# Moving a fold of the attention probabilities from VectorE to GpSimd in seven of eight batches

## The chip, the cores and the metric

The kernel runs on one core of one Trainium2 chip. The metric is the device time of one execution in microseconds (us), as the median of three runs. Engines are named as the profile names them: PE (TensorE matmul), PEld (TensorE weight load), DVE (VectorE), ACT (ScalarE), POOL (GpSimd), SP (SyncE, which here only starts DMAs).

## The reference, cut to what matters

The inputs are q, k, v (8 batches, 8 heads, 576 tokens, 64 values) and phi (32 memory slots for each token). An attention layer is followed by a Fourier mixing and a two-layer network:

```python
a = softmax(phi)                                 # over the 32 slots
k_m, v_m = a^T k, a^T v                          # 32 memory rows for each head
attn = softmax(q k_m^T / 8)                      # 576 x 32 for each head
x = (attn @ v_m) laid out as (8, 576, 512)
u = x + real(fft(fft(x, axis=1), axis=2))
un = (u - mean) / sqrt(var + 1e-6)
out = u + relu(un @ w_ch1) @ w_ch2               # 512 -> 2048 -> 512
```

The real part of the two-dimensional transform is made as matmuls with cosine and sine tables. Along the tokens it needs, of the probabilities `attn`, sums and differences of token t with token 576 - t, and again of those with their mirror at a quarter of the length. These sums and differences are the fold that the change is about.

## The kernel before, in words

**Two streams of work.** The network runs in 18 chunks of 256 tokens, each in 8 steps: `ffn1` (48 matmuls `ph`, 128x256) makes a slice of the hidden layer, ACT and DVE split it into two f16 halves (L940, L941, tile `hring`), and `ffn2` (24 matmuls `po`, 128x512) adds it into two PSUM banks. Chunk 0 is made in f32 with the raw weights while these are still being converted (`ffn1_direct`, `ffn2_direct`: `ph` at L894, ACT eviction L897, `po` at L911). The last chunks use another form of the second product. Beside that a generator, `background`, makes the attention and the mixing of the 8 batches, one step of it after each step of the network. Batch 0 stands before the network; batch 1 falls into chunks 0 and 1; batches 2 to 7 follow one by one until about 770 us.

**A batch of the background.** Heads are handled in four pairs. For b >= 2 `pooling_weights` turns phi into the tile `et` by way of `elt` and a DMA transpose (L419 on ACT, L420 on DVE, then `et<-elt`). Per pair `pair_memory` splits k and v into f16 halves and makes the memories (matmuls `pm`), and `pair_scores` makes the scores (matmuls `psc`) and their softmax in the tile `aring`. After the fourth pair come `values` (matmuls `pv`) and `spectrum` (matmuls `pa`, L741 and L749), then the mixing (`pp`, `px`).

**The end of `pair_scores`, which the change edits.** For b >= 1: POOL normalises (L635, 128x384); ACT and POOL make the two f16 halves of the first ten blocks (L647, L648); POOL makes the first level of the fold (L650, twice 128x128); DVE makes the second level in the tile `eo` (L652, L656, and L653, which has a per-partition mask in column 65 of `mk`); ACT casts `eo` to f16 (L659, tile `aeo`); POOL makes eight blocks of the low half (L660) and DVE the other four (L661, with the mask in column 64). The first matmul of `spectrum` reads those four blocks. In batch 0 DVE also does the work of L635 and L650.

**What sets the order.** The program is written for a scheduler that places each instruction on its engine's queue by a timeline of its own; engines then run their queues strictly in order. So an edit at one place can move rows of all engines at others.

Of the kernel before, what the change touches and what calls it, by code (L numbers as in the profile page):

```python
# [16 lines left out]
ALU = mybir.AluOpType  # L17
# [3 lines left out]
P = 128  # L21
B, H, S, D, M = 8, 8, 576, 64, 32
# [115 lines left out]
def kernel(  # L138
# [10 lines left out]
    nc = tc.nc  # L149
# [27 lines left out]
    mk = small[:, 0:68]  # L177
# [75 lines left out]
    def tiny(tag, n, bufs=2):  # L253
        if tag not in rings:
            rings[tag] = [taken[0], 0]
            taken[0] += n * bufs
        o, i = rings[tag]
        rings[tag][1] += 1
        o += i % bufs * n
        assert taken[0] <= 464, taken  # L260
        return scratch[:, o : o + n]
# [51 lines left out]
    def groups():  # L313

        last = [None]

        def mm(out, lhsT, rhs, start, stop):
            with tc.issue_after(last[0].ins) if start and last[0] is not None else nullcontext():
                m = nc.tensor.matmul(out, lhsT=lhsT, rhs=rhs, start=start, stop=stop)  # L319
            if stop:  # L320
                last[0] = marks["pe"] = m

        return mm
# [271 lines left out]
    def pair_scores(b, g, q, sc, km, es, aeo):  # L595

        n = f"{b}_{g}"
        psc = psg.tile([P, 512], F32, tag="g", name=f"psc_{n}")
        mm = groups()
        if b < NX:  # L600
            for t in range(6):
                mm(psc[:, t * 64 : t * 64 + 64], lhsT=q[:, t * P : (t + 1) * P], rhs=km, start=True, stop=True)
        else:
            nc.scalar.activation(qs[0], q, AF.Copy, scale=sc[:, 0:1])
            nc.vector.scalar_tensor_tensor(
                out=qs[1], in0=q, scalar=sc[:, 0:1], in1=qs[0], op0=ALU.mult, op1=ALU.subtract
            )
        for t in range(6) if b >= NX else ():
            for i, (qa, ka) in enumerate(((0, 0), (1, 0), (0, 1))):
                mm(  # L610
                    psc[:, t * 64 : t * 64 + 64],
                    lhsT=qs[qa][:, t * P : (t + 1) * P],
                    rhs=km[:, ka],
                    start=(i == 0),
                    stop=(i == 2),
                )
        pv = psc[:, 0:384].rearrange("p (c m) -> p c m", m=M)
        mx = tiny("smx", 12, 2)
        nc.vector.tensor_reduce(out=mx, in_=pv, axis=AX.X, op=ALU.max)  # L619
        a2, eo = aring[:, (b * NG + g) % NA], eot  # L620
        if b == 0 and g > 1:
            a2 = unring.rearrange("p a l t k c -> p (a l t k c)").bitcast(F32)[:, 640 * (g - 2) : 640 * (g - 1)]
            a2 = a2.rearrange("p (t m) -> p t m", m=M)
        if b == 0 and 0 < g < 3:
            eo = un.rearrange("p t c -> p (t c)")[:, 384 * (g - 1) : 384 * g]
            eo = eo.rearrange("p (t e c) -> p t e c", e=2, t=3)
        a = a2[:, :12]
        nc.vector.tensor_tensor(out=a, in0=pv, in1=mx.unsqueeze(2).to_broadcast([P, 12, M]), op=ALU.subtract)  # L628
        nc.scalar.activation(a, a, AF.Exp, scale=es)  # L629
        sm = tiny("ssm", 12, 2)  # L630
        nc.vector.tensor_reduce(out=sm, in_=a, axis=AX.X, op=ALU.add)
        nc.vector.tensor_scalar(out=sm, in0=sm, scalar1=1e-9, scalar2=2.0**-13, op0=ALU.add, op1=ALU.mult)
        nc.vector.reciprocal(out=sm, in_=sm)  # L633
        eng = nc.gpsimd if b else nc.vector
        eng.tensor_tensor(out=a, in0=a, in1=sm.unsqueeze(2).to_broadcast([P, 12, M]), op=ALU.mult)  # L635

        av = a.rearrange("p (t h) m -> p t (h m)", h=2)
        ahl = ahring[:, (b * NG + g) % NAH]
        if b == 0 and g > 0:
            ahl = ud.rearrange("p l t c -> p (l t c)")[:, (g - 1) * 5 * P : g * 5 * P]  # L640
            ahl = ahl.rearrange("p (t c) -> p t c", t=5)
        if b == 0:
            nc.scalar.copy(out=ahl[:, :, 0:64], in_=av[:, 0:5])
            nc.gpsimd.tensor_tensor(out=ahl[:, :, 64:128], in0=av[:, 0:5], in1=ahl[:, :, 0:64], op=ALU.subtract)
        else:
            ahl = ahs[:, g % 2]
            nc.scalar.copy(out=ahl[:, :, 0::2], in_=a[:, :10].unsqueeze(2).to_broadcast([P, 10, 2, M]))  # L647
            nc.gpsimd.tensor_tensor(out=ahl[:, :, 1], in0=a[:, :10], in1=ahl[:, :, 0], op=ALU.subtract)  # L648
        for i, op in ((12, ALU.add), (16, ALU.subtract)):
            eng.tensor_tensor(out=a2[:, i : i + 4], in0=a[:, 0:4], in1=a[:, 4:8], op=op)  # L650
        ap = a2[:, 8:].rearrange("p (t s h) m -> p t s (h m)", s=2, h=2)
        nc.vector.tensor_tensor(out=eo[:, 1:3, 0], in0=ap[:, 1:3, 0], in1=ap[:, 1:3, 1], op=ALU.add)  # L652
        nc.vector.scalar_tensor_tensor(  # L653
            out=eo[:, 0, 0], in0=ap[:, 0, 0], scalar=mk[:, 65:66], in1=ap[:, 0, 1], op0=ALU.mult, op1=ALU.add
        )
        nc.vector.tensor_tensor(out=eo[:, :, 1], in0=ap[:, :, 0], in1=ap[:, :, 1], op=ALU.subtract)  # L656
        hi, lo = (aeo[:, l].rearrange("p t e h c -> p (t e h) c")[:, :, g * M : g * M + M] for l in range(2))
        eov = eo.rearrange("p t e (h m) -> p (t e h) m", m=M)
        marks[f"a{b}_{g}"] = nc.scalar.copy(out=hi, in_=eov)  # L659
        nc.gpsimd.tensor_tensor(out=lo[:, 4:], in0=eov[:, 4:], in1=hi[:, 4:], op=ALU.subtract)  # L660
        marks[f"s{b}_{g}"] = nc.vector.scalar_tensor_tensor(  # L661
            out=lo[:, :4], in0=hi[:, :4], scalar=mk[:, 64:65], in1=eov[:, :4], op0=ALU.mult, op1=ALU.add
        )

        return ahl

# [502 lines left out]
    marks = {}  # L1169
# [6 lines left out]
    def background():  # L1176
# [3 lines left out]
        for b in range(B):  # L1180
# [7 lines left out]
            if b == 0:  # L1188

                for g in range(NG + 1):  # L1190
                    if g < NG:
                        km = memory_f32(b, g, first[g], vmf, [0])
                        mem[g] = first[g][:, KV:], None, km, 1.0 / 8.0
                    if g > 0:
                        ahl[g - 1] = pair_scores(b, g - 1, *mem.pop(g - 1), aeo)
                for g in range(NG):
                    memory_f32(b, g, first[g], vmf, [1])
            for step in range(NG + 2) if b > 0 else ():
                if step < NG:
                    r = load_pair(b, step)  # L1200
                if step >= 2:
                    pair_transpose(b, step - 2, ahl.pop(step - 2), attnT)
                if 0 <= step - 1 < NG:
                    ahl[step - 1] = pair_scores(b, step - 1, *mem.pop(step - 1), aeo)
                    yield (nt if half_made is None else half_made), 0
                if step < NG:
                    mem[step] = pair_memory(b, step, r, vmf, ivs)
                    yield (nt if half_made is None else half_made), 0
# [44 lines left out]
    for g in range(NG):  # L1253
        with tc.issue_after(marks["q"].ins):
            marks["q"] = nc.sync.dma_start(
                out=phi_next[:, :, g], in_=raw[1, g, :, KV:KVP].rearrange("p (t c) -> p t c", t=NST)
# [203 lines left out]
```

## Time and profile before

| | |
|---|---|
| median of 3 runs | 921.37 us (920.95 to 921.78) |
| the profiled execution | 921.82 us, of which the span from the first to the last instruction 920.0 us |
| PE busy | 908.0 us, 99% of the span |
| DVE, ACT, POOL busy | 618.9, 492.9, 268.4 us |
[...]

Read first how much of the span PE works, then where it waits and for whom, then the engines at those places. An engine that is half idle can still be the one that ends such a wait, since each runs its own queue in order.

### The profile page before, as it was taken

The page shows a single profiled execution, that of the slowest core. Times are in us where ns is not written, and L with a number is a line of the kernel's source. Part 1 is how long each engine was busy: PE and PEld are TensorE (multiplying, and loading weights), DVE is VectorE, ACT ScalarE, POOL GpSimd, SP SyncE. Part 2 cuts the span into 40 slices and gives each one's busy share as a digit, 9 for nine tenths or more (in the row PEclk, how much of TensorE's full clock was granted, in tenths as well). Part 3 has the DMA queues.
Part 4 walks back from the last instruction along what each step waited for, and adds up shares of the span by engine and source line. Part 5 has one row for each costly group of instructions (what it writes and reads, how often), then busy time and mean ns, then how long its engine had stood idle before and what let it go on. Part 6 is the DMA issues. An engine that isn't in the chain of part 4 may idle for free.

```text
span 920.0 us, 19352 instructions
## 1 busy us (share of the span) xinstructions
PE 908.0 (99%) x7796; PEld 670.4 (73%) x7796; DVE 618.9 (67%) x1471; ACT 492.9 (54%) x955; POOL 268.4 (29%) x302
## 2 busy tenths in 40 slices
PE   9999899999999999999999999999999999999998
PEld 8976567667766676666766667676676767688887
DVE  5979967686668766777634876766665866554554
ACT  5658867655455555655434464655556544533331
POOL 1304524232154413372160431162222421300000
PEclk9999999999999999999999999999999999999999
DMA  9958841454245261454124425165425443210000
GB/s 327 413 172 285 212 90 24 98 130 107 41 107 122 70 146 34 123 155 137 20 69 89 117 75 141 25 141 125 96 49 110 103 131 106 47 46 2 24 14 34
DMA packets 132761, 100.16 MB, mean 109 GB/s; under 512 B 115008, under 2 KB 115264, under 8 KB 130624
## 3 DMA queue, kind: packets, MB, share of 16 engines
q1 hardware_dynamic: 132672, 98.93, 40.4%
q8 instruction: 61, 1.00, 0.4%
q14 instruction: 28, 0.23, 0.1%
HBM read 62.35 MB, written 13.63 MB: 83 GB/s over the span
## 4 chain that ended last, share of the span: by engine, by line
PE 87%; DVE 6%; ACT 4%; issue 1%; DMA 1%; POOL 0%; ACTq 0%; SPq 0%; POOLq 0%
PE ph L319 36%; PE po L950 29%; PE po L1012 6%; PE pp_t L319 2%; PE pm L319 2%; PE psc L319 2%; PE po L911 1%; PE pa L749 1%; PE ph L894 1%; PE px_t L319 1%; PE idle L297 1%; PE pm L498 1%; DMA et<-elt 1%; PE pp_t L800 1%; DVE w2s L1101 1%
## 5 line engine op out<-in xcount | busy, mean ns | idle before, releaser
L319 PE MATMUL ph<-unring,w1t 128*128 128x256 f16 x3264 | 389.3, 273 | 0.0
L319 PEld LDWEIGHTS <-w1t 128*128 128x128 f16 x3264 | 313.8, 98 | 60.7 <-issue 2.7
L950 PE MATMUL po<-w2s,hring 128*128 128x512 f16 x1344 | 311.6, 379 | 0.0
L950 PEld LDWEIGHTS <-hring 128*128 128x128 f16 x1344 | 129.5, 98 | 130.7 <-issue 0.4
L941 DVE SCALAR_TENSOR_TENSOR hring<-ph,hring 128x512 f16<-128x512 f32 x112 | 76.2, 682 | 39.2 <-ACT hring L940 37.9
L940 ACT ACTIVATE hring<-ph 128x512 f16<-128x512 f32 x112 | 65.9, 588 | 48.8 <-PE ph L319 48.7
L635 POOL TENSOR_TENSOR aring<-aring,scratch 128x384 f32<-128x384 f32 x28 | 25.6, 916 | 181.7 <-DVE scratch L633 152.4
L860 POOL TENSOR_TENSOR scratch<-scratch,small 128x1 f32<-128x1 f32 x36 | 22.5, 627 | 180.9 <-DVE scratch L859 152.9
L881 POOL TENSOR_TENSOR ud<-un,ud 128x1024 f16<-128x1024 f32 x17 | 37.9, 2228 | 31.0 <-ACT ud L880 31.0
L629 ACT ACTIVATE aring<-aring,scratch 128x384 f32<-128x384 f32 x24 | 14.7, 611 | 55.7 <-DVE aring L628 55.7
L319 PEld LDWEIGHTS <-stg 128*128 128x128 f16 x912 | 35.5, 97 | 8.3 <-issue 4.0
L659 ACT CAST aeo<-eo 128x384 f16<-128x384 f32 x30 | 15.4, 512 | 43.4 <-DVE eo L656 43.4
L619 DVE TENSOR_REDUCE scratch<-psc 128x12 f32<-128x384 f32 x32 | 17.6, 551 | 26.0 <-PE pm L319 18.7
L836 DVE SCALAR_TENSOR_TENSOR uring<-px_t,scratch,share 128x256 f32<-128x256 f32 (+1 forms) x80 | 34.2, 477 | 0.9 <-PE px_t L319 0.8
L647 ACT CAST at<-aring 128x640 f16<-128x640 f32 x28 | 20.3, 724 | 25.1 <-POOL aring L635 25.1
L911 PE MATMUL po<-w2s,hring 128*128 128x512 f32 x64 | 31.2, 610 | 2.0 <-ACT hring L897 2.0
L1034 POOL TENSOR_TENSOR uring<-uring,share 128x256 f32<-128x256 f32 x3 | 2.2, 728 | 105.9 <-ACT share L1031 105.9
L650 POOL TENSOR_TENSOR aring<-aring 128x128 f32<-128x128 f32 x56 | 31.7, 586 | 2.0
L894 PE MATMUL ph<-unring,w1t 128*128 128x256 f32 x128 | 30.6, 383 | 0.0
L652 DVE TENSOR_TENSOR eo<-aring 128x128 f32<-128x128 f32 x29 | 26.7, 919 | 4.9 <-POOL aring L650 4.9
L894 PEld LDWEIGHTS ph<-unring,w1t 128*128 128x128 f32 x128 | 23.9, 190 | 7.7 <-issue 5.0
L854 ACT ACTIVATE un<-uring 128x512 f32<-128x512 f32 x32 | 20.0, 624 | 17.5 <-POOL ud L881 8.7
(324 smaller groups left out, 1544.3 us busy)
## 6 DMA issues: line engine op xcount, KB each, us to landing
out<-uring SPq DMA_DIRECT2D x35, 256.0 KB, 2.1
rawt<-in_raw SPq DMA_DIRECT2D x13, 640.0 KB, 4.5
stg<-in_raw SPq DMA_DIRECT2D x13, 640.0 KB, 5.1
stg<-in_w SPq DMA_DIRECT2D x7, 1024.0 KB, 6.4
rawt<-in_raw SPq DMA_DIRECT2D x15, 384.0 KB, 3.2
stg<-in_raw SPq DMA_DIRECT2D x15, 384.0 KB, 3.1
w2s<-in_w SPq DMA_DIRECT2D x4, 1024.0 KB, 10.5
kept_t<-ud SPq DMA_DIRECT2D x8, 512.0 KB, 2.6
```

The lines of the kernel that those rows point to most:

```text
L319: m = nc.tensor.matmul(out, lhsT=lhsT, rhs=rhs, start=start, stop=stop)
L635: eng.tensor_tensor(out=a, in0=a, in1=sm.unsqueeze(2).to_broadcast([P, 12, M]), op=ALU.mult)
L650: eng.tensor_tensor(out=a2[:, i : i + 4], in0=a[:, 0:4], in1=a[:, 4:8], op=op)
L652: nc.vector.tensor_tensor(out=eo[:, 1:3, 0], in0=ap[:, 1:3, 0], in1=ap[:, 1:3, 1], op=ALU.add)
L836: nc.vector.scalar_tensor_tensor(out=u[rows, hs], in0=px[rows, hs], scalar=igx[rows], in1=tm[rows, w * NJ + half : w * NJ + half + 256], o ...
L881: marks[f"ul{c}"] = nc.gpsimd.tensor_tensor(out=ud[:, 1], in0=un, in1=ud[:, 0], op=ALU.subtract)
L894: nc.tensor.matmul(ph, lhsT=w[:, k, f * P : (f + 1) * P], rhs=unTs[0][:, k], start=(k == 0), stop=(k == NK - 1))
L911: nc.tensor.matmul(po[t], lhsT=h[:, f, t], rhs=w[:, f], start=(j == 0 and f == 0), stop=(j == NW - 1 and f == UB - 1),)
L940: marks["fa"] = nc.scalar.activation(h[:, 0], phv, AF.Relu)
L941: marks["fd"] = nc.vector.scalar_tensor_tensor(out=h[:, 1], in0=phv, scalar=0.0, in1=h[:, 0], op0=ALU.max, op1=ALU.subtract)
L950: nc.tensor.matmul(po[t], lhsT=hs[j][:, lh, f * 2 + t], rhs=w2s[:, j * UB + f, lw, :], start=(j == 0 and f == 0 and i == 0), stop=(j == NW ...
L1012: m = nc.tensor.matmul(po[n], lhsT=h[:, la, a], rhs=b[lb], start=(j == 0 and i == 0 and n in ("p1", "p6", "p5", "p4")), stop=(j == NW - 1 ...
```

## The change

In batches 1 to 7 the whole fold is made by POOL. Two instructions change engine as they are (L652 and L656). The two that multiply by a mask and add in one instruction become two each: for L653 a multiplication with the mask, spread over 64 columns, and an addition; for L661 a multiplication into four blocks of `aring` that are no longer needed, and an addition. Batch 0 stays on DVE. DVE loses 4 instructions for each of 28 pairs (112), POOL gains 6 (168). The number of matmuls stays the same.

```diff
-        nc.vector.tensor_tensor(out=eo[:, 1:3, 0], in0=ap[:, 1:3, 0], in1=ap[:, 1:3, 1], op=ALU.add)
-        nc.vector.scalar_tensor_tensor(
-            out=eo[:, 0, 0], in0=ap[:, 0, 0], scalar=mk[:, 65:66], in1=ap[:, 0, 1], op0=ALU.mult, op1=ALU.add
-        )
-        nc.vector.tensor_tensor(out=eo[:, :, 1], in0=ap[:, :, 0], in1=ap[:, :, 1], op=ALU.subtract)
+        eng.tensor_tensor(out=eo[:, 1:3, 0], in0=ap[:, 1:3, 0], in1=ap[:, 1:3, 1], op=ALU.add)
+        eng.tensor_tensor(out=eo[:, :, 1], in0=ap[:, :, 0], in1=ap[:, :, 1], op=ALU.subtract)
+        if b:
+            eng.tensor_tensor(
+                out=eo[:, 0, 0], in0=ap[:, 0, 0], in1=mk[:, 65:66].to_broadcast([P, 2 * M]), op=ALU.mult
+            )
+            eng.tensor_tensor(out=eo[:, 0, 0], in0=eo[:, 0, 0], in1=ap[:, 0, 1], op=ALU.add)
+        else:
+            nc.vector.scalar_tensor_tensor(
+                out=eo[:, 0, 0], in0=ap[:, 0, 0], scalar=mk[:, 65:66], in1=ap[:, 0, 1], op0=ALU.mult, op1=ALU.add
+            )
...
-        marks[f"s{b}_{g}"] = nc.vector.scalar_tensor_tensor(
-            out=lo[:, :4], in0=hi[:, :4], scalar=mk[:, 64:65], in1=eov[:, :4], op0=ALU.mult, op1=ALU.add
-        )
+        if b:
+            part = a[:, 8:12]
+            nc.gpsimd.tensor_tensor(
+                out=part, in0=hi[:, :4], in1=mk[:, 64:65].unsqueeze(2).to_broadcast([P, 4, M]), op=ALU.mult
+            )
+            nc.gpsimd.tensor_tensor(out=lo[:, :4], in0=part, in1=eov[:, :4], op=ALU.add)
```

Lines behind the edit stand 13 lower in the changed file (L894 becomes L907, L897 L910, L911 L924, L741 L754, L749 L762, L880 L893, L730 L743).

**POOL, the last pair of a batch.** First the queue of before, from the normalisation to the low half:

```order
L635 TENSOR_TENSOR aring<-aring,scratch 128x384
L650 TENSOR_TENSOR aring<-aring 128x128 x2
L648 TENSOR_TENSOR at<-aring,at 128x10x32
L660 TENSOR_TENSOR aeo<-eo,aeo 128x8x32
L860 TENSOR_TENSOR scratch<-scratch,small 128x1 x2
```

The same place in the changed kernel:

```order
L635 TENSOR_TENSOR aring<-aring,scratch 128x384
L650 TENSOR_TENSOR aring<-aring 128x128 x2
L655 TENSOR_TENSOR eo<-aring,small 128x64
L648 TENSOR_TENSOR at<-aring,at 128x10x32
L652 TENSOR_TENSOR eo<-aring 128x2x64
L653 TENSOR_TENSOR eo<-aring 128x3x64
L658 TENSOR_TENSOR eo<-eo,aring 128x64
L666 TENSOR_TENSOR aeo<-eo,aeo 128x8x32
L669 TENSOR_TENSOR aring<-aeo,small 128x128
L672 TENSOR_TENSOR aeo<-aring,eo 128x4x32
L873 TENSOR_TENSOR scratch<-scratch,small 128x1 x2
```

Six rows have come in; four of them (L655, L652, L653, L658) stand ahead of ACT's cast and two behind it, where L661 stood on DVE.

**PE, the start of batch 1's spectrum** (`ph_7` and `po` are the last step of chunk 0, `pa` is the spectrum, `ph_0` the first step of chunk 1). Before:

```order
L894 MATMUL ph_7_0_1333<-unring,w1t 128x256
L894 MATMUL ph_7_1_1339<-unring,w1t 128x256 x4
L741 LDWEIGHTS aeo
L741 MATMUL pa_0_0_1250<-ct,aeo 128x290
...
L749 MATMUL pa_0_1_1260<-ct,aeo 128x145
L911 MATMUL po_0_736<-w2s,hring 128x512
L741 LDWEIGHTS aeo
L741 MATMUL pa_1_0_1270<-ct,aeo 128x290
```

In the changed kernel:

```order
L907 MATMUL ph_7_0_1341<-unring,w1t 128x256
L907 MATMUL ph_7_1_1347<-unring,w1t 128x256 x4
L924 MATMUL po_0_736<-w2s,hring 128x512
L924 MATMUL po_1_737<-w2s,hring 128x512
L319 LDWEIGHTS w1t
L319 MATMUL ph_0_1437<-unring,w1t 128x256
...
L924 MATMUL po_0_736<-w2s,hring 128x512
L754 LDWEIGHTS aeo
L754 MATMUL pa_0_0_1258<-ct,aeo 128x290
```

Three `po` and 16 `ph` now stand ahead of the spectrum; the two halves of the spectrum that stood ahead of the first `po` now stand behind the third.

**ACT, the start of batch 7** (L410 and L411 the exponentials of phi, L542 and L604 the first pair's splits, L880 the cast that belongs to a chunk's normalisation, L419 the write of `elt`). Before:

```order
L880 CAST ud<-un 128x1024
L410 ACTIVATE phs,scratch<-pf_0_8216,scratch 128x512
L411 ACTIVATE phs,scratch<-pl_8215,scratch 128x64
L410 ACTIVATE phs,scratch<-pf_1_8223,scratch 128x512
L542 ACTIVATE stg<-rawt,scratch 128x5x128
L604 ACTIVATE stg<-rawt,scratch 128x768
L854 ACTIVATE un,scratch<-uring 128x512
L419 ACTIVATE elt<-phs,scratch 128x576
```

In the changed kernel:

```order
L868 ACTIVATE un,scratch<-uring,scratch 128x512 x2
L410 ACTIVATE phs,scratch<-pf_0_8264,scratch 128x512
L411 ACTIVATE phs,scratch<-pl_8263,scratch 128x64
L410 ACTIVATE phs,scratch<-pf_1_8271,scratch 128x512
L542 ACTIVATE stg<-rawt,scratch 128x5x128
L604 ACTIVATE stg<-rawt,scratch 128x768
L893 CAST ud<-un 128x1024
L419 ACTIVATE elt<-phs,scratch 128x576
```

The cast L880 (now L893) has moved from ahead of the exponentials to just ahead of L419.

## Rows read from the trace of the kernel before

**Rows 1.** The page, busy us of each engine, share, instructions

```profile
PE 908.0 (99%) x7796; PEld 670.4 (73%) x7796; DVE 618.9 (67%) x1471; ACT 492.9 (54%) x955; POOL 268.4 (29%) x302
```

**Rows 2.** Busy time by stretch: us, engines busy (x instructions), PEclk, DMA, GB/s

```profile
460.00:770.00 310.00, 310.00 (x2720) 217.61 (x2719) 203.34 (x476) 162.30 (x328) 100.42 (x109) 1.00 0.42 102
```

**Rows 3.** What PE waited for: us in total, times, longest

```profile
PE pm L319 <- DMA et<-elt: 2.1, 2, 1.4
PE po L911 <- ACT hring L897: 2.0, 3, 1.4
PE pv L722 <- ACT share L703: 1.7, 1, 1.7
...
PE psc L319 <- ACT scratch L587: 1.0, 1, 1.0
PE pa L741 <- DVE aeo L661: 0.2, 1, 0.2
```

**Rows 4.** Groups by shape on DVE: busy us, mean ns, idle before

```profile
L652 DVE TENSOR_TENSOR eo<-aring 128x128 f32<-128x128 f32 x29 | 26.7, 919 | 4.9 <-POOL aring L650 4.9
L661 DVE SCALAR_TENSOR_TENSOR aeo<-aeo,small,eo 128x128 f16<-128x128 f16 x30 | 23.3, 778 | 7.8 <-ACT aeo L659 7.8
L656 DVE TENSOR_TENSOR eo<-aring 128x192 f32<-128x192 f32 x29 | 17.9, 618 | 0.0
L653 DVE SCALAR_TENSOR_TENSOR eo<-aring,small 128x64 f32<-128x64 f32 x29 | 16.6, 572 | 8.4 <-POOL aring L635 8.4
```

**Rows 5.** Groups by shape on POOL, the costliest of the fold

```profile
L650 POOL TENSOR_TENSOR aring<-aring 128x128 f32<-128x128 f32 x56 | 31.7, 586 | 2.0
```

**Rows 6.** POOL in order of time, last pair of batch 5: start, us

```profile
564.50 0.83 POOL L635 TENSOR_TENSOR aring<-aring,scratch 128x384 f32<-128x384 f32 x1 [10.38 <-DVE scratch L633]
565.40 0.87 POOL L650 TENSOR_TENSOR aring<-aring 128x128 f32<-128x128 f32 x2
566.23 0.79 POOL L648 TENSOR_TENSOR at<-aring,at 128x320 f16<-128x320 f32 x1
568.06 0.67 POOL L660 TENSOR_TENSOR aeo<-eo,aeo 128x256 f16<-128x256 f32 x1 [1.04 <-ACT aeo L659]
```

**Rows 7.** DVE in order of time, the same pair

```profile
568.02 0.86 DVE L661 SCALAR_TENSOR_TENSOR aeo<-aeo,small,eo 128x128 f16<-128x128 f16 x1 [0.58 <-ACT aeo L659]
```

**Rows 8.** PE in order of time, from there to batch 5's spectrum

```profile
565.12 2.78 PE L319 MATMUL ph<-unring,w1t 128*128 128x256 f16 x24
567.74 2.75 PE L950 MATMUL po<-w2s,hring 128*128 128x512 f16 x12
570.43 0.29 PE L741 MATMUL pa<-ct,aeo 128*128 128x290 f16 x1
```

**Rows 9.** ACT in order of time, batch 1's last pair

```profile
120.21 0.51 ACT L659 CAST aeo<-eo 128x384 f16<-128x384 f32 x1
122.63 0.64 ACT L897 ACTIVATE hring<-ph 128x256 f32<-128x256 f32 x2
```

**Rows 10.** POOL in order of time, batch 1's last pair

```profile
116.99 0.83 POOL L635 TENSOR_TENSOR aring<-aring,scratch 128x384 f32<-128x384 f32 x1 [3.70 <-DVE small L288]
```

**Rows 11.** PE in order of time, batch 1's spectrum

```profile
121.38 0.30 PE L741 MATMUL pa<-ct,aeo 128*128 128x290 f16 x1 [0.17 <-DVE aeo L661]
123.05 1.12 PE L911 MATMUL po<-w2s,hring 128*128 128x512 f32 x2 [0.45 <-ACT hring L897]
```

**Rows 12.** ACT in order of time, start of batch 7

```profile
692.18 1.04 ACT L880 CAST ud<-un 128x1024 f16<-128x1024 f32 x1 [2.01 <-DVE un L861]
704.19 0.77 ACT L419 ACTIVATE elt<-phs,scratch 128x576 f16<-128x576 f32 x1 [3.11 <-DMA et<-elt]
```

**Rows 13.** PE in order of time, start of batch 7

```profile
705.27 0.70 PE L319 MATMUL pm<-et,stg 128*128 128x64 f16 x20
```

**Rows 14.** POOL in order of time, start of batch 4

```profile
365.71 2.13 POOL L961 TENSOR_TENSOR un<-w2s 128x1024 f32<-128x1024 f16 x1
```

**Rows 15.** DVE in order of time, start of batch 4

```profile
366.12 3.01 DVE L548 SCALAR_TENSOR_TENSOR stg<-rawt,scratch,stg 128x320 f16<-128x320 f32 x2
```

More of the change, by code (lines that the diff above doesn't have):

```diff
@@ L660, in pair_scores @@
         nc.gpsimd.tensor_tensor(out=lo[:, 4:], in0=eov[:, 4:], in1=hi[:, 4:], op=ALU.subtract)
-        marks[f"s{b}_{g}"] = nc.vector.scalar_tensor_tensor(
-            out=lo[:, :4], in0=hi[:, :4], scalar=mk[:, 64:65], in1=eov[:, :4], op0=ALU.mult, op1=ALU.add
-        )
+        if b:
[4 more added lines that the diff above has]
+            nc.gpsimd.tensor_tensor(out=lo[:, :4], in0=part, in1=eov[:, :4], op=ALU.add)
+        else:
+            nc.vector.scalar_tensor_tensor(
+                out=lo[:, :4], in0=hi[:, :4], scalar=mk[:, 64:65], in1=eov[:, :4], op0=ALU.mult, op1=ALU.add
+            )
         return ahl
```

## Prediction

> **What bounds the kernel now.** Read first the page's busy times: PE works 908.0 of 920.0 us [rows 1]. Then the table of stretches: from 460 to 770 us, where batches 5 to 7 are made beside the network, PE is busy in all of 310.00 us [rows 2], while DVE works 66% and POOL 32% of it. The kernel is a queue of matmuls with almost no gap, and the change adds or takes no matmul. So its time can move only by what PE waits. Third, PE's waits [rows 3]: besides 1.6 us at the very start they add up to 7.0 us, and they say where to look. The waits for L897 (the eviction of chunk 0), for L703 and for L661 fall into batch 1; the two for `et<-elt` (1.4 and, as the rest of 2.1, 0.7 us) at the starts of batches 4 and 3; the one for L587 in batch 3. Relief for DVE can win back some of these 7.0 us and no more; POOL, which gets longer chains, can add waits anywhere.
>
> The profiled execution took 921.82 us, 0.45 above the median of 921.37; I work on the former and move the result by that.
>
> **What leaves DVE and what POOL gets.** By their means the four instructions cost DVE 0.92 + 0.78 + 0.62 + 0.57 = 2.89 us for a pair [rows 4], 81 us over 28 pairs. Since DVE ends few of PE's waits, these 81 us are not time won. POOL gets six instructions. The trace has none of these forms; the nearest row is L650, 128x128, at 0.59 us by its mean [rows 5] and 0.87/2 = 0.44 us undisturbed [rows 6]. I take 0.44 for the three with 128 elements, 0.55 for 192 (between 0.44 and the 0.67 of L660 with 256), 0.35 for the two with 64 (below the 0.44 of twice the width; 0 to 0.59 are its bounds). Together 2.6 us for a pair; with L650's mean for all of them 3.5. That is 72 to 98 us on an engine with 650 us free, so the load doesn't matter, only the latency does.
>
> **The last pair of batches 2 to 7** decides when the spectrum can start. Batch 5 stands for all six. POOL's L635 starts at 564.50, the two L650 end at 566.27 [rows 6], DVE's L661 ends at 568.02 + 0.86 = 568.88 [rows 7], and PE starts the spectrum at 570.43 [rows 8]: 1.55 us of slack. In the changed order I add up behind 566.27: 0.35 (mask), 0.79 (L648, which stands in between), 0.44, 0.55, 0.35, then ACT's cast 0.51, then 0.67 for L660 and 0.44 twice, and some 0.35 of handoffs between them: 4.9 us, so 571.16. The fold ends 2.3 us later than before. But the order of PE also moved: between the fourth `psc` and the first `pa` stand 56 `ph` and 24 `po` where 37 and 24 stood, 19 more at 0.109 us (24 took the 2.62 us from 565.12 to 567.74 [rows 8]), so 2.1 us. Slack left: 1.55 + 2.1 - 2.3 = 1.35 us. The same reading, row by row, gives slacks of 1.9, 2.0, 0.7, 1.55, 1.9 and 1.8 us in batches 2 to 7; the cover grows by 10, 12, 14, 19, 10 and 13 `ph` and in batches 4 and 7 also by 5 and 3 `po` (0.215 us: 12 and one `ph` fill 567.74 to 570.43). What is left is 0.7, 1.0, 1.0, 1.35, 0.7 and 1.55 us. Cost: nothing, but the cover is thin, and gone in batches 2 and 6 once the added chain takes 3.0 us instead of 2.3.
>
> **Batch 1.** Before, PE starts the spectrum at 121.38, works on its first half until 122.60, and waits 0.45 us for ACT's L897, until 123.05 [rows 11]. In the changed order both `po` that need L897 stand first and that first half behind them, so PE has nothing to do until L897. L897 stands on ACT behind the cast of `eo`, with 123.05 - 120.21 = 2.84 us from the cast's start to PE's start [rows 9, 11]. The cast now waits for POOL: from L635 at 116.99 [rows 10] 0.83, 0.94 (two L650 and the handoff), 0.21 for a small memset between them, 0.35, 0.44, 0.55, 0.35 and 0.15 of handoffs make 120.8, which is 0.6 later than 120.21. So `po` starts 0.6 later, and the spectrum's first half (1.22 us) is then still to do: 1.8 us lost. Against it stands what brings L635 itself forward, since DVE has less to do in the three pairs before. The place is PE's wait of 1.7 us for L703, whose inputs come from DVE behind L652 and L656 of the third pair, at most 0.92 + 0.62 = 1.5 us [rows 3, 4]. Bounds: 0, and the waits ahead of this place, 2.0 + 1.7 - 0.45 = 3.25. I take 0.9, nearer to the 1.5 than to 3.25, because ACT is in that chain too. Net: +0.9, between -1.5 and +1.8. The fold itself is not late there: behind the cast (120.8) come 0.8 for L648, 0.7 for L660, 0.5 for the mask, 2.1 for a 1024-wide POOL row that stands ahead of the last addition (as L961 [rows 14]) and 0.4 for that, 125.4 with handoffs, while PE has three f32 `po` and 16 `ph`, about 3.0 us, from 123.65 to 126.7.
>
> **The starts of batches 3, 4 and 7**, where the new order moves other rows. PE's first `pm` there needs `et`, and `et` needs ACT's L419 and DVE's L420. *Batch 7:* the transpose is in at 704.19, since then ACT's second L419 may go on [rows 12], and PE's `pm` starts at 705.27 [rows 13]: 1.08 us of slack. In the changed order PE has 8 `po` less and 1 `ph` more ahead of it, 1.6 us less cover. On ACT the cast L880 (1.04 us) has moved behind the exponentials, which may start about 0.9 us sooner, but now it stands just ahead of L419, and the 1024-wide POOL instruction behind it runs beside L420, which has two inputs in SBUF. What that means is seen at batch 4's start: L548 starts 0.41 us after POOL's L961, which lasts 2.13 us, and two of them take 3.01 us [rows 14, 15]. Gain and hold-up nearly cancel; I make it +0.15 us for the chain. 1.6 + 0.15 - 1.08 = 0.7 us of new wait. *Batch 3:* the same move of L880, but here POOL's L961 also moves behind the time of L548, whose hold-up goes (in batch 4, where the two stand in the same way, from 366.12 to 365.71 + 2.13 = 367.84, so 1.7 us [rows 14, 15]); cover falls by 5 `po` and 1 `ph`, 1.2 us. The 0.7 us of waiting should go: -0.7. *Batch 4:* cover falls by 0.8, the chain by about as much: 0. *L587 in batch 3:* six more `ph` stand ahead of the `psc` that waited 1.0 us: -0.6.
>
> [...] The trace shows DVE instructions with two SBUF inputs that last longer beside a POOL instruction [rows 14, 15], and L652 with 128 elements at a mean of 0.92 us where L656 with 192 takes 0.62 [rows 4]. [...]
>
> **Sum:** +0.9 - 0.7 - 0.6 + 0.7 = +0.3: 922.1 against 921.82, so a median of 921.7 us. I forecast no change that can be told: a measurement here can tell about 0.2% (1.8 us).
>
> **Rivals.** *Faster (0.22):* DVE is what holds batch 1 back, and L635 of its last pair comes 3.25 us sooner: -1.45 there, and with the waits at the starts of batches 3 and 4 and the one for L587 gone (-0.7, -1.4, -1.0) and none new, -4.6 us: 916.8. For it speaks that three of five waits end in batch 1; against it that ACT and POOL stand in the same chain. *Slower, the spectrum late (0.18):* the fold's chain takes 1.5 us more than I took. It decides from 0.7 us on; at 1.5 more the waits are 0.8, 0.5, 0.5, 0.15, 0.8 and 0, and batch 1 pays 0.9 more: +3.7 and the forecast's 0.3, 925.4. For it speaks L650's mean, a third over its undisturbed time, which alone gives 0.8; against it that the rows which hold POOL up were the ones that leave DVE. [...] *No change (0.50):* my forecast, 920 to 923.2.
>
> **Numbers.** Faster 0.22, same 0.50, slower 0.28. The range goes from 918.5 (half of the faster case) to 925.5 (either slower case); the forecast's own range is 920 to 923.2.
>
> **What would show it.** Right: DVE's busy time down by about 80 us, POOL's up by 70 to 100; PE's matmuls the same number; PE's wait at batch 1's spectrum now for L897 (its line now L910) and about 2 us long; no wait of `pa` in batches 2 to 7; a wait for `et` of about 0.7 us at batch 7's start and none at batch 3's. Wrong: `pa` waiting for POOL's last fold row, or waits of PE in rows that have none now, `px` above all, since the order moved everywhere and I went only through the groups named here.

## The result: slower, 1.0096 times the time before

| | before | changed |
|---|---|---|
| median, us | 921.58 (920.95 to 922.04) | 930.53 (929.75 to 930.92) |
| ratio, 95% interval | 1 | 1.0096 [1.0076, 1.0116] |
| span of the profiled execution, us | 920.0 | 929.0 |

The forecast was 921.7 us and no difference that can be told. Some executions are disturbed, with a long half-clock stretch in the prologue (a granted clock of 0.52 from 22 to 61 us in the first profile of the changed kernel): times given here are medians of the others, the rows of the changed kernel come from a second, undisturbed profile of it (span 929.0 us, mean granted clock 0.994; the kernel before: 1.000), and of the two profiles below that are disturbed (batch 1 alone, and the one-column rows in the changed kernel) only rows behind the prologue are read.

A *row* is an instruction in the profile. A row is called *held* where it lasts much longer than others of its form and ends with a row of another engine that runs beside it.

### The profile page after: what moved, and what is told of

Its sections match the earlier page's. It is cut to its first block, busy times and chain, and to the rows that moved or that the text cites. A ratio compares the mean times of both kernels' runs of the same rounds, so it can differ in the third digit from the quotient of the medians.

```text
span 946.8 us, 19422 instructions
## 1 busy us (share of the span) xinstructions
PE 929.7 (98%) x7796; PEld 690.1 (73%) x7796; DVE 552.7 (58%) x1359; ACT 493.7 (52%) x955; POOL 338.9 (36%) x470
## 4 chain that ended last, share of the span: by engine, by line
PE 89%; DVE 3%; POOL 2%; DMA 2%; ACT 2%; SPq 1%; issue 1%; ACTq 0%; DVEq 0%
PE ph L319 36%; PE po L963 29%; PE po L1025 6%; PE pm L319 3%; PE pp_t L319 2%; PE psc L319 2%; PE po L924 2%; PE pm L498 2%; PE ph L907 2%; PE pa L762 1%; DMA w1t<-in_raw 1%; PE px_t L319 1%; PE pv L735 1%; PE pp_t L813 1%; PE idle L297 1%
## 5 line engine op out<-in xcount | busy, mean ns | idle before, releaser
L953 ACT ACTIVATE hring<-ph 128x512 f16<-128x512 f32 x112 | 66.0, 590 | 63.6 <-PE ph L319 62.6
L635 POOL TENSOR_TENSOR aring<-aring,scratch 128x384 f32<-128x384 f32 x28 | 24.9, 891 | 132.4 <-DVE scratch L633 84.8
L894 POOL TENSOR_TENSOR ud<-un,ud 128x1024 f16<-128x1024 f32 x17 | 37.1, 2185 | 40.7 <-ACT ud L893 40.7
L924 PE MATMUL po<-w2s,hring 128*128 128x512 f32 x64 | 33.1, 639 | 3.4 <-ACT hring L910 3.3
L835 DVE SCALAR_TENSOR_TENSOR share<-pp_t,scratch,small 128x257 f32<-128x257 f32 (+1 forms) x48 | 21.1, 480 | 23.4 <-ACT small L832 23.3
L545 POOL TENSOR_TENSOR stg<-stg 128x640 f16<-128x640 f32 x12 | 20.4, 1699 | 35.3 <-ACT stg L544 23.5
L907 PE MATMUL ph<-unring,w1t 128*128 128x256 f32 x128 | 31.6, 392 | 0.0
L568 DVE TENSOR_REDUCE scratch<-pm 128x64 f32<-128x128 f32 x24 | 7.0, 291 | 42.0 <-PE pm L319 42.0
L650 POOL TENSOR_TENSOR aring<-aring 128x128 f32<-128x128 f32 x56 | 30.6, 566 | 1.6
```

Of the source, the lines that this page charges most:

```text
L894: marks[f"ul{c}"] = nc.gpsimd.tensor_tensor(out=ud[:, 1], in0=un, in1=ud[:, 0], op=ALU.subtract)
L907: nc.tensor.matmul(ph, lhsT=w[:, k, f * P : (f + 1) * P], rhs=unTs[0][:, k], start=(k == 0), stop=(k == NK - 1))
L924: nc.tensor.matmul(po[t], lhsT=h[:, f, t], rhs=w[:, f], start=(j == 0 and f == 0), stop=(j == NW - 1 and f == UB - 1),)
L953: marks["fa"] = nc.scalar.activation(h[:, 0], phv, AF.Relu)
```

## The profile after

The busy times on the page of the changed kernel, against [rows 1]:

```profile
PE 911.6 (98%) x7796; PEld 672.4 (72%) x7796; DVE 553.8 (60%) x1359; ACT 492.8 (53%) x955; POOL 339.1 (37%) x470
```

DVE lost 65 us of work, POOL gained 71, and neither shows in the time. What shows is that PE is busy 3.6 us longer with the same 7796 matmuls, and waits more. Its waits, against [rows 3] (us in total, times, longest):

```profile
PE po L924 <- ACT hring L910: 3.3, 3, 2.1
PE po L963 <- ACT hring L953: 3.2, 1, 3.2
PE pm L319 <- DMA et<-elt: 2.7, 2, 2.1
...
PE pv L735 <- ACT share L716: 1.2, 1, 1.2
...
PE po L1025 <- DVE uring L1070: 0.6, 1, 0.6
```

These make 11.0 us where the rows of before made 7.0. (Two more, 0.6 and 0.3 us for first loads, belong to the start.) So 4.0 of the 9.0 us are waits like those of before, and 0.9 are at the start. The rest is mostly in the clock. Busy time by stretch, as in [rows 2], in batch 1 and at the start of batch 4:

```profile
104.00:113.00 9.00, 7.68 (x34) 4.52 (x34) 7.44 (x19) 8.21 (x13) 8.84 (x10) 1.00 0.47 165
113.00:120.50 7.50, 5.54 (x9) 3.11 (x10) 4.58 (x12) 5.92 (x14) 7.34 (x14) 0.54 0.54 117
120.50:127.00 6.50, 6.50 (x35) 3.54 (x35) 1.29 (x2) 4.46 (x8) 4.52 (x6) 1.00 0.79 149
374.00:380.00 6.00, 6.00 (x53) 4.99 (x51) 4.88 (x9) 1.48 (x6) 5.47 (x4) 1.00 0.56 68
380.00:383.50 3.50, 0.38 (x3) 0.00 (x0) 2.13 (x6) 3.50 (x9) 1.67 (x3) 0.97 0.52 113
383.50:387.00 3.50, 3.43 (x16) 2.20 (x17) 3.50 (x5) 2.81 (x5) 1.40 (x1) 0.54 0.45 145
```

The number behind those of the five engines is the clock that PE was granted, as a share of its full clock: four `po` of batch 1 last 3.78 us in the stretch at 0.54 and four last 1.98 in the one at 1.00. The trace's clock records put the half level at 113.65 for 6.83 us and at 383.31 for 3.41 us. Both begin inside a wait of PE, and 1.31 and 0.26 us of them still belong to that wait. In the other 5.52 and 3.15 us PE works at half speed, which costs half of them, 2.8 and 1.6 us. That is an estimate; the rows agree (four `po` and six `ph` of batch 1 last 3.78 and 2.42 us where four and six at full clock last 1.98 and 1.46), and PE's busy time, which counts rows that overlap once, grew by 3.6. Waits, start and clock, 4.0 + 0.9 + 4.4 = 9.3, account for the 9.0 us.

**Batch 1.** PE in order of time:

```profile
112.29 0.41 PE L735 MATMUL pv<-hring,share 64*32 64x512 f16 x8 [1.16 <-ACT share L716]
112.64 0.20 PE L270 MATMUL as_sq<-scratch,small 128*128 128x1 bf16 x2
114.96 3.78 PE L924 MATMUL po<-w2s,hring 128*128 128x512 f32 x4 [2.12 <-ACT hring L910]
118.54 2.42 PE L907 MATMUL ph<-unring,w1t 128*128 128x256 f32 x6
...
121.43 1.98 PE L924 MATMUL po<-w2s,hring 128*128 128x512 f32 x4
```

Two waits, 1.16 and 2.12 us, with 0.55 us of work between, and then four `po` take 3.78 us; the same four take 1.98 at 121.43. In the kernel before, PE waits once at this place, 1.68 us for L703, and the same four `po` follow without a wait, at full clock:

```profile
113.00 1.96 PE L911 MATMUL po<-w2s,hring 128*128 128x512 f32 x4
```

What the second wait waits for is seen on POOL, DVE and ACT (third pair of batch 1):

```profile
106.14 2.14 POOL L1138 TENSOR_TENSOR w1t<-w1t 128x1024 f16<-128x1024 f32 x1
108.23 1.02 POOL L635 TENSOR_TENSOR aring<-aring,scratch 128x384 f32<-128x384 f32 x1
...
110.93 1.43 POOL L652 TENSOR_TENSOR eo<-aring 128x128 f32<-128x128 f32 x1
112.33 1.03 POOL L653 TENSOR_TENSOR eo<-aring 128x192 f32<-128x192 f32 x1
113.32 0.76 POOL L658 TENSOR_TENSOR eo<-eo,aring 128x64 f32<-128x64 f32 x1
```

```profile
110.66 1.39 DVE L1140 SCALAR_TENSOR_TENSOR w1t<-w1t,small 128x1024 f16<-128x1024 f32 x1
```

```profile
114.12 0.51 ACT L665 CAST aeo<-eo 128x384 f16<-128x384 f32 x1 [1.88 <-POOL eo L658]
114.53 0.38 ACT L910 ACTIVATE hring<-ph 128x256 f32<-128x256 f32 x1
```

ACT's cast stands ahead of the eviction L910, whose `ph` had ended by 111.13 (a PE row of 1.89 us from 109.24), and now waits 1.88 us for the last row of POOL's fold, which stands behind a 2.14 us row for the weights, L1138. L652 takes 1.43 us instead of its mean of 0.49: DVE's L1140 runs beside it. Before, the cast of this pair waited for nothing:

```profile
111.41 0.51 ACT L659 CAST aeo<-eo 128x384 f16<-128x384 f32 x1
```

**The start of batch 4.** DVE, POOL, ACT and PE:

```profile
374.37 2.06 DVE L405 TENSOR_TENSOR scratch<-scratch 128x2 f32<-128x2 f32 x1
377.08 1.56 DVE L406 TENSOR_SCALAR scratch<-scratch 128x2 f32<-128x2 f32 x1
```

```profile
374.29 2.12 POOL L894 TENSOR_TENSOR ud<-un,ud 128x1024 f16<-128x1024 f32 x1 [1.74 <-ACT ud L893]
376.49 2.12 POOL L974 TENSOR_TENSOR un<-w2s 128x1024 f32<-128x1024 f16 x1
```

```profile
378.74 0.69 ACT L410 ACTIVATE phs<-pf,scratch 128x512 f32<-128x512 f32 x1 [4.52 <-DVE scratch L291]
...
382.92 0.59 ACT L953 ACTIVATE hring<-ph 128x512 f16<-128x512 f32 x1
```

```profile
383.57 1.04 PE L963 MATMUL po<-w2s,hring 128*128 128x512 f16 x2 [3.19 <-ACT hring L953]
```

Two DVE rows with *two numbers per partition* take 2.06 and 1.56 us, where the median of their six is 0.16: each ends, at 376.43 and 378.64, with the 1024-wide POOL row it stands beside (374.29 + 2.12 = 376.41, 376.49 + 2.12 = 378.61). ACT idles 4.52 us for them; the eviction L953 is queued on ACT behind the exponentials (L410, L411) and three scalings (L542, L604); PE waits 3.19 us for it, and half clock follows. None of these rows is part of the change: both wide POOL rows were there before, but the moment moved. In the kernel before, both DVE rows had ended when the first wide row started at 363.51:

```profile
362.27 0.15 DVE L405 TENSOR_TENSOR scratch<-scratch 128x2 f32<-128x2 f32 x1
...
362.46 0.17 DVE L406 TENSOR_SCALAR scratch<-scratch 128x2 f32<-128x2 f32 x1
```

## Experiments

**The changed kernel once more.** No edit.

> The changed kernel once more, for a profile without the long stretch of half clock that its first profile has between 23 and 60 us. Theory A (the loss sits in places where the new order makes PE wait: batch 1, for L910; the starts of batches 2 and 4; and in the half clock that follows two of these waits): about 930.5 us, half clock near 10 us in all, in one stretch behind batch 1's wait and one behind batch 4's. Theory B (every batch's fold comes late and costs about 1.3 us): about 930.5 us too, but with a wait of the spectrum's first matmul in each batch.

Measured: 930.9 us (930.27 to 931.2), 1.0098 [1.0084, 1.0111]. All four executions have a mean clock of 0.994: the loss and the half-clock stretches come back each time.

**The change in batch 1 alone, and in batches 2 to 7 alone.** Theory A: a few places, batch 1 and the start of batch 4, make the loss. Rival, theory B: each batch's fold is late. The edit, for the first (for the second `b > 1` in both places):

```
-        eng.tensor_tensor(out=eo[:, 1:3, 0], ...)
+        fold = nc.gpsimd if b == 1 else nc.vector
+        fold.tensor_tensor(out=eo[:, 1:3, 0], ...)
...
-        if b:
+        if b == 1:
             part = a[:, 8:12]
```

> The fold on POOL in batch 1 alone; batches 2 to 7 keep it on DVE. The start of batch 4 has the queue order of the kernel before, batch 1's that of the changed kernel. Theory A: PE's wait for L910 with its half clock (about 4 us) and the wait for et at batch 2's start (1.9 us) stay, the wait at batch 4's start goes: about 927. Theory B: one seventh of the loss, about 922.9.

> The fold on POOL in batches 2 to 7, batch 1 keeps it on DVE. Batch 1's queues stand as in the kernel before, batch 4's start as in the changed kernel. Theory A: only the wait at batch 4's start with its half clock is new (about 4.9 us, against 1.4 of wait there before), and two waits of batch 3 go (1.7): about 924. Theory B: six sevenths of the loss, about 929.5.

Measured: batch 1 alone 926.65 us (926.20 to 927.08), 1.0053 [1.0039, 1.0066], as theory A has it; batches 2 to 7 alone 920.77 (920.08 to 921.44), 0.9991 [0.9982, 1.0000], where theory A expected about 924. Six batches on POOL, 24 of the 28 pairs, cost nothing as long as batch 1 stays on DVE; four pairs cost 5 us. The two parts don't add up to the 9 us: the stall with half clock at batch 4's start comes in neither. In the kernel with batch 1 alone the pattern of batch 1 stands as in the changed kernel, waits of 1.21 and 2.08 us and then half clock (four `po` in 3.78 us). In the one with batches 2 to 7 the clock is full throughout, and batch 4's start shows why it got away:

```profile
367.36 0.16 DVE L405 TENSOR_TENSOR scratch<-scratch 128x2 f32<-128x2 f32 x1
...
368.19 1.52 DVE L406 TENSOR_SCALAR scratch<-scratch 128x2 f32<-128x2 f32 x1
```

```profile
367.56 2.13 POOL L895 TENSOR_TENSOR ud<-un,ud 128x1024 f16<-128x1024 f32 x1 [2.03 <-ACT ud L894]
```

Here L405 starts 0.20 us *ahead* of the wide row and takes 0.16 us; only L406 is held. PE's wait for the eviction is 1.27 us, and the clock stays full. Theory B falls; of theory A the places stand, but whether batch 4's start stalls hangs on some 0.3 us in the start of two rows.

**The two held rows written as one-column rows**, in the changed kernel. DVE's rows of one column there are short throughout (L872, 36 rows, 0.13 to 0.16 us).

```
-        nc.vector.tensor_tensor(out=mx[:, 0:2], in0=mx[:, 0:2], in1=mx[:, 2:4], op=ALU.max)
-        nc.vector.tensor_scalar(out=mx[:, 0:2], in0=mx[:, 0:2], scalar1=-1.0, scalar2=None, op0=ALU.mult)
+        for g in range(2):
+            m = mx[:, g : g + 1]
+            nc.vector.tensor_scalar(out=m, in0=m, scalar1=mx[:, 2 + g : 3 + g], scalar2=-1.0, op0=ALU.max, op1=ALU.mult)
```

> The changed kernel, with the two-column instructions L405 and L406 of pooling_weights (a maximum of two SBUF tiles, a factor -1) replaced by two one-column tensor_scalar instructions that do both with a scalar operand. In the changed kernel's first profile L405 lasts 2.06 us and L406 1.55 us at batch 4's start beside 1024-wide POOL instructions, and PE waits 3.2 us there. [...] If the hold is not the cause there: about 930.5 as before.

Measured: 926.3 us (926.09 to 927.93), 1.0054 [1.0039, 1.0069], and not the 930.5 of the case in which the hold is not the cause. Batch 4's wait is 1.12 us, with full clock; batch 1's 2.13 us and its half clock stay. The order at batch 4 is still the bad one, with POOL's wide row ahead, and the new one-column row, 0.09 us behind it, isn't held; the three-column row that comes next is:

```profile
391.58 2.13 POOL L895 TENSOR_TENSOR ud<-un,ud 128x1024 f16<-128x1024 f32 x1 [1.74 <-ACT ud L894]
```

```profile
391.67 0.21 DVE L407 TENSOR_SCALAR scratch<-scratch 128x1 f32<-128x1 f32 x1
391.80 1.94 DVE L288 TENSOR_SCALAR scratch<-scratch 128x3 f32<-128x3 f32 x1
```

So some 4 us of the 9 go with the held rows, most of them at batch 4 (2.1 of wait and 1.6 of clock; the wait for `et` at batch 2's start is 1.05 us here instead of 2.14, and one of 0.75 is new at batch 4). Batch 1 makes most of the rest.

**Which part of the fold matters in batch 1.** The changed kernel with, in batch 1 only, the second level back on DVE (`fold = nc.gpsimd if b > 1 else nc.vector`), or the masked low half back on DVE (`if b > 1:` ahead of `part`).

> The changed kernel, but in batch 1 only the masked low half is on POOL; the second level of the fold (three instructions) is back on DVE there. Theory A: batch 1's loss comes from ACT's cast of eo, which stands ahead of L910 and waits for POOL's four second-level rows; with these back on DVE there is no new wait and no half clock in batch 1: about 921, or up to 925 where batch 4's start falls out as badly as in the changed kernel. Rival: it comes from the sum of POOL's added work in batch 1; then a third of the 5 us stays even with a good batch 4: about 922.5, with a wait for L910 of more than 1.4 us.

> The mirror of it: the changed kernel, but in batch 1 the masked low half is back on DVE, and the second level stays on POOL. Theory A: batch 1 keeps its wait of about 2.1 us for L910 and the half clock behind it, so some 4 us of loss: 925 to 929, by how batch 4's start falls out. Rival: two thirds of batch 1's 5 us, 924 with a good batch 4.

Measured: second level back: 929.0 us (928.8 to 929.23), 1.0079 [1.0064, 1.0093]; hardly a gain, and a miss. The third pair's wait went, but one of 2.30 us for the same eviction (its line is L911 here) came up at 123.0, with half clock for 3.41 us from 126.29, and batch 4's wait (3.25 us) and its 3.41 us of half clock stayed:

```profile
122.45 0.51 ACT L666 CAST aeo<-eo 128x384 f16<-128x384 f32 x1
...
124.87 0.65 ACT L911 ACTIVATE hring<-ph 128x256 f32<-128x256 f32 x2
```

```profile
125.29 2.83 PE L925 MATMUL po<-w2s,hring 128*128 128x512 f32 x4 [2.30 <-ACT hring L911]
```

This wait isn't one for POOL: the cast waits for nothing, and ACT works without a gap from 116.17 until the eviction. Before, ACT's rows at this place were the same and PE waited 0.45 us [rows 11], since it had the spectrum's first half to do; here that half stands behind these `po`. It is what the prediction described for batch 1's spectrum, brought about by PE's order.

Low half back: 924.3 (922.67 to 926.47), 1.0031 [1.0019, 1.0043]. Theory A missed here too, since it expected batch 1's wait of 2.1 us and its half clock to stay; the rival's 924 is met, but not its condition, a good batch 4. Here POOL's third pair starts 1.02 us sooner, since the two rows of the pair before are gone from its queue (against 106.14 and 108.23 above):

```profile
104.19 2.44 POOL L1139 TENSOR_TENSOR w1t<-w1t 128x1024 f16<-128x1024 f32 x1 [0.65 <-ACT w1t L1138]
107.21 0.83 POOL L635 TENSOR_TENSOR aring<-aring,scratch 128x384 f32<-128x384 f32 x1 [0.57 <-DVE scratch L633]
```

The second wait in batch 1 is 1.44 us instead of 2.12 and the clock stays full there in this profile; batch 4 keeps its 3.17 us and 3.41 us of half clock. The executions of this one kernel differ with the clock: 922.67 us at a mean of 1.000, 923.85 to 924.48 at 0.997 and 0.998, 926.34 and 926.47 at 0.994. The instructions are the same, so up to 3.8 us go with the clock.

**The one-column rows where no stall is.** In the kernel with batches 2 to 7 alone, and in the kernel before.

> The fold on POOL in batches 2 to 7 alone, and the two-column maximum of pooling_weights replaced by one-column instructions. Theory A with the hold: the 1.3 us that PE waits at batch 4's start and the 0.4 us for et go: about 919.3. Rival (the order moves with each edit, and with it the waits): other waits take their place, 920 to 922.

> The kernel before with the same replacement of the two-column maximum and nothing else. Its two waits for et (2.1 us in all) stand behind that chain: theory A about 919.7; where L405 and L406 were not held in the kernel before (0.16 and 0.17 us in its trace at batch 4's start) the gain is what the two rows and the order give, 0 to 1 us: 921.

Measured: 921.2 us, 0.9998 [0.9989, 1.0006], the rival's case, and 924.7 (923.9 to 925.59), 1.0033 [1.0020, 1.0046], a miss. The second is a loss from an edit that was meant only to take cost away from DVE: two waits for `et`, 2.35 and 2.41 us, stand where the kernel before has 0.74 and 1.40, with full clock in the profile. The edit moved other rows in the queues. So the gain of the same edit in the changed kernel may also hold such moves; that the held rows were the cause there rests on the rows shown above.

**Both remedies together, and the parts alone in all batches.** The low half of batch 1 on DVE with the one-column rows; only the second level on POOL; only the low half on POOL.

> The kernel whose batch 1 keeps the masked low half on DVE, and with it the two-column maximum and its sign written as one-column rows. Theory A (what is left of the loss there is the start of batch 4 alone: the two-column rows L405 and L406 held by 1024-wide POOL rows, 2.06 and 1.55 us, then PE's wait of 3.17 us and a half-clock stretch of 3.41 us): the one-column rows are not held, the wait is 1.3 us or less and no half-clock stretch follows; 922.7 less 1.9 less 1.7 makes 919 us, range 918 to 920.5. Rival (the wait at batch 4 comes from POOL's longer queue, whoever is held): the wait stays near 3 us and the time near 922.7. Third way (the edit moves other rows, as it did in the kernel before, where two waits for et of 2.4 us came up): waits for et, 921 to 925.

> Only the fold's second level on POOL in batches 1 to 7, the masked low half on DVE in all of them. Theory A: batch 1 goes as in the kernel that keeps the low half on DVE there alone (waits of 1.3 and 1.4 us, no half clock, no loss to speak of); the loss then hangs on the start of batch 4 alone: 922 to 923.5 if POOL's first 1024-wide row starts ahead of L405, 919 to 921 if it starts behind. Rival (each POOL row added costs something, half of them cost half): 926.

> Only the masked low half on POOL in batches 1 to 7, the second level on DVE in all of them. Theory A: the stalls are a matter of where single rows fall, and the number of POOL rows decides nothing: batch 1 goes as in the kernel that keeps the second level on DVE there alone (a wait near 2.3 us for L910's form, a half-clock stretch of 3.41 us, some 3 to 4 us lost), batch 4 as its first wide row falls: 923 to 929. Rival (each POOL row added costs something; two of the six rows are added, so a third of the loss): 924, with waits spread over the batches and no half-clock stretch.

Measured: together 922.8 us, 1.0014 [1.0004, 1.0024]: a miss. Batch 4 did what was expected, a wait of 1.13 us and full clock (ahead of the exponentials only one row is held now, the three-column L288, 1.94 us); but batch 1, with waits of 1.31 and 1.45 us, nearly as when the low half alone was back, fell to half clock this time:

```profile
113.00:119.00 6.00, 4.97 (x18) 2.70 (x20) 4.15 (x13) 5.31 (x12) 5.16 (x9) 0.72 0.59 109
```

Executions of it at a mean clock of 1.000 took 921.73 to 922.8 us, at 0.998 and 0.996 923.06 to 925.49. Second level only: 924.0 us, 1.0019 [1.0007, 1.0031], above the 923.5 expected at most; only L405 is held at batch 4 (2.06 us), the wait there 0.87 us; batch 1 has 1.34 and 1.44 us again, and half clock for 6.83 us. Low half only: 925.4, 1.0041 [1.0028, 1.0054], within theory A's range; a wait of 2.55 us in batch 1, at the same place and with the same order of PE as the 2.30 us above, and 3.41 us of half clock; at batch 4 L405 alone is held (2.06 us) and the wait is 0.45 us. In both kernels the longest waits and the half clock stand at single places, as theory A has it, and not spread by the number of added rows. But the half clock behind 1.3 and 1.4 us of waiting, in the first and the second of these kernels, was not expected.

No version beats the kernel before by more than can be told; the change in batches 2 to 7 alone comes nearest, at 0.9991 [0.9982, 1.0000].

## Why the prediction was wrong

It failed on **two terms of the sum**: the start of batch 4, priced at 0, was worth 3.4 us, and batch 1, priced at +0.9, was worth 3.4. A third was not in the sum at all: the start of batch 2, 2.1 us. At batch 4 the wait itself was missed, since the evictions queued on ACT were not followed; at both places a wait was priced by its length alone, and half clock, which cost 4.4 us in all, had no term.

- *What leaves DVE, what POOL gets.* POOL gained 71 us, within "70 to 100". DVE lost 65 where "about 80" was expected: the fold's own rows fell by 82, but other rows lengthened (the 13 two-column rows with two inputs from 2.3 to 6.4 us), and busy time counts overlapping rows once. The six rows were put at 2.6 us for a pair; their means add up to 2.83 (0.33, 0.49, 0.63, 0.38, 0.54, 0.45). None of this shows in the time.
- *The last pair of batches 2 to 7.* "Cost: nothing": right, no `pa` waits for the fold, and batches 2 to 7 alone measure 0.9991. The rival "the spectrum late" falls with it. Against it stood that the DVE rows which hold POOL up were leaving; L650's mean stayed at 0.57 us (0.59 before), and its longest pair of before, 2.44 us at 514.75, ran beside L972 and L605, which stay on DVE.
- *Batch 1.* A wait for L910 of about 2 us was named as a sign, and one of 2.12 us came, but the number is luck: it was worked out for the spectrum, where PE waits for nothing now, and it came a pair earlier, at the third pair's cast. The mechanism, a cast that waits for POOL ahead of the eviction, is the one forecast. The waits of the batch went from 3.89 to 4.50 us, +0.6 against +0.9. (The first of them shrank from 1.38 to 0.62 us, since PE came there 0.8 us later, after longer waits for the start's loads.) What was missed is the clock: 6.83 us at half clock, worth 2.8. The relief that was counted on (L635 of the last pair sooner) didn't come: it starts at 117.34 where it started at 116.99, behind POOL's own queue, in which the extra rows of each pair push the wide L1138 and the next pair's L635 back.
- *Batch 4's start.* "cover falls by 0.8, the chain by about as much: 0." Only `et` was followed there. The wait for `et`, 1.40 us, did go; in its place PE waits 3.19 us for L953, which stands on ACT behind exponentials that wait for L405 and L406. That is +1.8 us of wait and 1.6 of clock. The prediction had followed wide DVE rows beside 1024-wide POOL rows (L548 at the starts of batches 3 and 4, L420 at batch 7's), not the `128x2` rows; the POOL rows that held these, 2.1 us each, are old ones, at another moment. L405 starting 0.08 us behind the wide row takes 2.06 us, and starting 0.20 us ahead of it, in the kernel with batches 2 to 7 alone, 0.16. No run varied that offset alone.
- *Batch 2's start.* Not in the sum. PE waits 2.14 us for `et` there, where it waited for nothing before. DVE's L405 is held on the way (1.47 us, beside a 2.13 us POOL row), and ACT's exponentials wait 1.22 us behind it. The rest of the delay was not traced.
- *Batch 3.* The wait for L587 (1.0 us) went, where -0.6 was predicted; that for `et` fell from 0.74 to 0.52 where -0.7 was expected. *Batch 7.* The 0.7 us of new wait didn't come; one of 0.6 us for L1070 did, at 823 us in the network's last chunks.

In waits the changed kernel lost some 4 us (0.6 + 2.1 + 1.8 + 0.6 - 0.2 - 1.0 = 3.9), against the +0.3 of the sum; the clock and the start made it 9. Waits "in rows that have none now" were among the prediction's own signs of being wrong; two of these came (L953 at batch 4, `et` at batch 2). Shown: that batch 1's part is needed for all of the loss, that batches 2 to 7 alone cost nothing, and that the held rows at batch 4 set PE's wait there. Argued from the order of events only: that the idle time of PE is what lowered its clock. A kernel that fills the waits with other matmuls, and nothing else moved, was not tried. Open: why the same two waits of 1.3 and 1.4 us in batch 1 are followed by half clock in one kernel and not in another, why executions of one kernel differ in it, and which of POOL's rows in batch 1 matter, since each edit there also moved PE's order.

## What to carry to other kernels

Where one engine is a queue without gaps, price a new wait twice: by its length, and by the clock behind it, which here cost 2.8 and 1.6 us on top of two waits of 3.3 (1.16 and 2.12, close together) and 3.2 us, and nothing behind one of 2.1 us. When an edit moves POOL's queue, look first for the short DVE rows of two or three columns that feed ACT (held here for 1.5 to 2.1 us, instead of 0.16), and for the wide POOL rows that can come to stand just ahead of them; at each start of a batch follow every eviction that is queued behind them, not only the operand that PE waited for before. Moving work off the busier engine was worth nothing by itself here: 65 us left DVE, and the best part of the change measures 0.9991.

## What the runs showed of the hardware

- Tiny rows were held: `128x2` rows of DVE took 0.16 us or, beside a 1024-wide POOL row, 2.06, 1.56 and 1.52 us, and a `128x3` row 1.94, each to within 0.03 us of the end of that POOL row. A one-column row (`128x1`, L407) that started 0.09 us behind such a POOL row took 0.21 us. The other way round, POOL's L652 (`128x128`) took 1.43 us instead of 0.49 beside a `128x1024` row of DVE.
- PE's wait at batch 4 goes with how many of the two rows are held: two held, 3.17 to 3.25 us (three kernels); one held, 0.45 to 1.27 us (three kernels).
- PE's clock fell to half in the second of two waits of 1.16 and 2.12 us 0.55 us apart (for 6.83 us), in a wait of 3.19 us (for 3.41 us), and in some executions behind 1.3 + 1.4 us; it stayed full behind single waits of 2.14, 2.35 and 2.41 us, but not behind single ones of 2.30 and 2.55 (3.41 us of it, from 1.0 and 0.2 us behind their end). With the low half of batch 1 on DVE, one and the same kernel took 922.67 us at a mean clock of 1.000 and 926.47 at 0.994. No run here isolates what sets the moment at which the clock changes.
